# The opening of a fused attention and mixture kernel, with the order of each engine written out

## The chip, the cores and the metric

The kernel runs on one core of a Trainium2 chip. The metric is the device time of one execution in microseconds, lower is better. The time before the change is 762.0 us, the median of three runs (761.38 to 763.36). A core has TensorE (PE, matrix products and transposes), VectorE (DVE), ScalarE (ACT), GpSimd (POOL) and a sync engine (SP) that issues the DMAs. Each works through its own list in order and waits on semaphores where an input comes from another.

## The reference

Three layers in a row, all in fp32. Attention with keys and values pooled over 8 positions (8 batches, 8 heads, 576 positions, 64 wide), then a layer with squared relu, then a soft mixture of 8 experts:

```
k_p = k.reshape(B, H, Sp, 8, D).mean(axis=3)       # v_p likewise, Sp = 72
scores = scale * q @ k_p.T                          # per batch and head
attn = softmax(scores)
x = (attn @ v_p) as [4608 tokens, 512]
h = x @ w_in                                        # 512 x 2048, stored as 64-bit floats
x = relu(h)**2 @ w_out                              # 2048 x 512, 64-bit floats too
logits = x @ phi                                    # 512 x 32 slots
d = softmax(logits over tokens); slot_input = d.T @ x
slot_out[e] = relu(slot_input[e] @ w1[e]) @ w2[e]
out = softmax(logits over slots) @ slot_out
```

## The kernel before

Tokens are worked in 36 tiles of 128. Tile t goes through attention in steps: `att_qT` (four PE transposes of q, L218, copied by ACT, L222, into the one buffer `acc`), `att_sc` (scores on PE, L234; maxima on DVE, L241; eight exponentials with sums on ACT, L245; for tiles 2, 14 and a few others DVE subtracts, L250, and `att_exp` does one exponential, L259), `att_norm` (DVE, L264 to L268), `att_aT` (PE transposes, L299, two ACT copies, L300), and `att_av` (values on PE, L311; ACT copies the result as a rounded part `xh`, L318; DVE takes the rest as `xl`, L319).

The first layer is worked in units (t, j): tile t by quarter j of w_in (512 columns). A unit is 12 matmuls (L452) in two halves of six: per 128 rows kk of the quarter, high times high, high times low, and low times high, so kk 0 and 1 are the first half, 2 and 3 the second. After it come relu (L465) and square (L474) on ACT, or the square on DVE, and a store of g to DRAM.

w_in arrives as 64-bit floats. Each chunk (j, kk), 128 x 512, is converted by `conv_steps` in four steps: ACT L342; DVE L344, L347, L351; DVE L355, L356; ACT L394 (the rounded part) and POOL L395 (the rest). The buffer `tmp` has eight slots, so L342 of a chunk waits for L395 of the third chunk before it. The loads of a quarter go into one of two staging tiles (quarter 2 into that of 0, quarter 3 into that of 1), freed by L351.

A planner of the framework orders each engine's instructions by their place in the program and a timeline that it simulates; `early` raises a call's priority, `behind`, `pinned` and `paced` put a call's instructions behind a marked instruction on that instruction's engine. Such an edge is an order in a list and no wait on the chip. In `opening()`, before, tile 0's steps are early, conversions of quarters 0 and 1 are cut into steps and put behind marks, and tiles 1 to 3 follow with the planner's order. Units start with (0, 0), and 2u and 2u + 1 are the slots of unit u; `at(slot, ...)` hangs a call on a slot. From slot 2 on hang the conversions of quarter 2 (`CS`, each behind the latest relu on ACT), then those of quarter 3, at slots 12 to 18 the k poolings of batch 1 (`pool_k`, 32 PE matmuls each, L164), at 20 to 26 its V poolings on DVE, at 24 tile 4's attention. The V of batch 0 is pooled chunk by chunk: two of the four on PE (`pool_v`, L182) and two on DVE (`pool_v_dve`, L189).

SP's list at the start is k of batch 0 (four loads), q of tile 0, two chunks of w_in, v (four), two chunks of w_in, q of tile 1, four chunks of quarter 1, q of tiles 2 and 3.

## Time and profile before

| | us |
|---|---|
| median of three runs | 762.0 |
| the profiled execution | 760.21 |
| its span, from first to last instruction | 758.4 |
| PE busy in it | 718.1 (95%) |
| DVE busy | 532.6 (70%) |
| ACT busy | 391.0 (52%) |
| POOL busy | 131.3 (17%) |
| mean granted clock of PE | 0.985 |

The busy share of each engine over the whole span says which one is the bound on average. PE's 95% leaves some 40 us; 13 of them lie in the first 60 us and 14 in the last 58. What a change in one stage is worth is read in that stage, from the busy time in a window, the timeline there, and what an instruction waited for before it began (in square brackets: the idle time of its engine and what ended it). Busy times count an instruction from start to end; instructions of one engine overlap by some 0.1 us in a dense list.

### The profile page before, as it was taken

The page shows a single profiled execution, that of the slowest core. Times are in us where ns is not written, and L with a number is a line of the kernel's source. Part 1 is how long each engine was busy: PE and PEld are TensorE (multiplying, and loading weights), DVE is VectorE, ACT ScalarE, POOL GpSimd, SP SyncE. Part 2 cuts the span into 40 slices and gives each one's busy share as a digit, 9 for nine tenths or more (in the row PEclk, how much of TensorE's full clock was granted, in tenths as well). Part 3 has the DMA queues.
Part 4 walks back from the last instruction along what each step waited for, and adds up shares of the span by engine and source line. Part 5 has one row for each costly group of instructions (what it writes and reads, how often), then busy time and mean ns, then how long its engine had stood idle before and what let it go on. Part 6 is the DMA issues. An engine that isn't in the chain of part 4 may idle for free.

```text
span 758.4 us, 14481 instructions
## 1 busy us (share of the span) xinstructions
PE 718.1 (95%) x5260; PEld 508.1 (67%) x5260; DVE 532.6 (70%) x1065; ACT 391.0 (52%) x1135; POOL 131.3 (17%) x151
## 2 busy tenths in 40 slices
PE   7589999999999999999999999999999999998993
PEld 7467788787776767676667666666666676663462
DVE  4996865397796788888888887788788746324153
ACT  2675577464756446346646552636674454341142
POOL 2232300004872400050351311220000000000000
PEclk9799999999999999999999999999999999999996
DMA  8965764658876987695998788788586436979988
GB/s 252 277 225 175 229 178 133 208 155 247 223 217 168 260 252 196 205 281 148 253 267 232 206 232 242 205 244 233 163 277 197 122 101 235 417 248 367 370 298 297
DMA packets 224135, 175.10 MB, mean 231 GB/s; under 512 B 75072, under 2 KB 186688, under 8 KB 224064
## 3 DMA queue, kind: packets, MB, share of 16 engines
q1 hardware_dynamic: 224064, 174.17, 76.1%
q8 instruction: 42, 0.69, 0.4%
q14 instruction: 29, 0.24, 0.1%
HBM read 126.94 MB, written 47.19 MB: 230 GB/s over the span
## 4 chain that ended last, share of the span: by engine, by line
PE 64%; DVE 16%; DMA 9%; ACT 5%; issue 2%; SPq 2%; POOL 1%; DVEq 0%; ACTq 0%; POOLq 0%
PE l L452 40%; PE misc L632 3%; PE pl L540 3%; PE misc L1100 2%; ACT es L245 2%; PE gT L311 2%; PE l L1068 2%; PE att L311 2%; DMA kv<-in_k_dram 2%; DMA st<-in_moe_w_in_dram 2%; PE gT L234 2%; DVE aT L286 2%; PE att L540 1%; DMA out_dram<-o 1%; PE att L164 1%
## 5 line engine op out<-in xcount | busy, mean ns | idle before, releaser
L452 PE MATMUL l<-w,xh 128*128 128x512 f32 x1152 | 380.4, 410 | 7.0 <-ACT xh L318 2.9
L452 PEld LDWEIGHTS l<-w,xh 128*128 128x128 f32 x1152 | 208.8, 189 | 72.9 <-issue 16.3
L452 PE MATMUL l<-w,xl 128*128 128x512 f32 x576 | 230.7, 401 | 0.7 <-DVE xl L319 0.7
L465 ACT ACTIVATE r<-l 128x512 f32<-128x512 f32 x144 | 86.3, 603 | 162.7 <-PE l L452 154.7
L452 PEld LDWEIGHTS l<-w,xl 128*128 128x128 f32 x576 | 108.8, 189 | 28.7 <-issue 3.4
L157 POOL TENSOR_TENSOR kv<-kv 72x512 f32<-72x512 f32 x40 | 54.1, 1357 | 224.7 <-DMA kv<-in_v_dram 115.9
L284 ACT COPY aT<-turned 32x256 f32<-32x256 f32 (+1 forms) x168 | 67.8, 404 | 21.1 <-DVE turned L293 19.1
L472 DVE TENSOR_TENSOR g<-l,r 128x512 f32<-128x512 f32 x57 | 38.8, 680 | 23.3 <-ACT r L465 15.1
L515 DVE STREAM_TRANSPOSE turned<-turned 128x1024 f32<-128x1024 f32 x39 | 47.5, 1229 | 3.8 <-DMA turned<-g_dram 3.8
L245 ACT ACTIVATE es<-att,mx 128x72 f32<-128x72 f32 x120 | 36.7, 331 | 21.7 <-DVE mx L241 21.4
L286 DVE COPY aT<-turned 32x256 f32<-32x256 f32 (+1 forms) x120 | 42.8, 356 | 1.7
L245 ACT ACTIVATE es<-gT,mx 128x72 f32<-128x72 f32 x120 | 36.8, 331 | 10.9 <-DVE mx L241 10.9
L474 ACT ACTIVATE g<-r 128x512 f32<-128x512 f32 x54 | 34.5, 640 | 0.8
L395 POOL TENSOR_TENSOR w<-tmp,w 128x512 fp32r<-128x512 f32 x16 | 22.8, 1426 | 67.4 <-ACT w L394 61.4
L472 DVE TENSOR_TENSOR tmp<-l,r 128x512 f32<-128x512 f32 x33 | 22.5, 682 | 16.3 <-ACT r L465 14.1
L515 DVE STREAM_TRANSPOSE tmp<-tmp 128x1024 f32<-128x1024 f32 x25 | 30.2, 1221 | 4.7 <-DMA tmp<-g_dram 4.7
L158 POOL TENSOR_TENSOR kv<-kv 72x256 f32<-72x256 f32 x40 | 32.7, 824 | 0.9
L344 DVE TENSOR_SCALAR tmp<-tmp 128x512 uint32<-128x512 uint32 x32 | 16.6, 517 | 21.5 <-ACT tmp L342 21.3
L342 ACT ACTIVATE tmp<-st 128x512 f32<-128x512 f32 x32 | 21.5, 676 | 17.6 <-DMA st<-in_moe_w_in_dram 13.3
L268 DVE TENSOR_TENSOR es<-es,rs 128x576 f32<-128x576 f32 x36 | 29.6, 824 | 0.8
L245 ACT ACTIVATION_READ_ACCUMULATOR es<-gT,mx 128x1 f32 x120 | 26.1, 217 | 0.0
L245 ACT ACTIVATION_READ_ACCUMULATOR es<-att,mx 128x1 f32 x120 | 26.0, 217 | 0.0
(203 smaller groups left out, 1058.8 us busy)
## 6 DMA issues: line engine op xcount, KB each, us to landing
g_dram<-g SPq DMA_DIRECT2D x95, 256.0 KB
turned<-g_dram SPq DMA_DIRECT2D x39, 512.0 KB
w<-in_moe_w_dram SPq DMA_DIRECT2D x32, 512.0 KB
tmp<-g_dram SPq DMA_DIRECT2D x25, 512.0 KB
w<-in_moe_w_dram SPq DMA_DIRECT2D x6, 2048.0 KB
g_back<-g_dram SPq DMA_DIRECT2D x40, 256.0 KB
kv<-in_k_dram SPq DMA_DIRECT2D x32, 288.0 KB
kv<-in_v_dram SPq DMA_DIRECT2D x32, 288.0 KB
```

Source lines behind the costliest of these rows:

```text
L157: eng.tensor_tensor(out=x[:, :, 0:4], in0=x[:, :, 0:4], in1=x[:, :, 4:8], op=ALU.add)
L158: eng.tensor_tensor(out=x[:, :, 0:2], in0=x[:, :, 0:2], in1=x[:, :, 2:4], op=ALU.add)
L245: mark["es", t] = nc.scalar.activation(out=es[:, e], in_=sv[:, h], func=AF.Exp, bias=mx[:, e:e + 1], accum_out=rsum[:, t % 8, e, 0:1],)
L284: nc.scalar.copy(out=dst, in_=src)
L286: eng[e].tensor_copy(dst, src)
L311: nc.tensor.matmul(px[e * D:(e + 1) * D, i * P + off:i * P + off + n], vp_t[b][:, 2 * i + e], aT[:, 2 * i + e, off:off + n],)
L452: mm = mark["l1", t, j] = nc.tensor.matmul(hp_t[t, j], steps[i][0], steps[i][1], start=(i == 0), stop=(i == 2 * n - 1))
L465: nc.scalar.activation(out=r, in_=hp, func=AF.Relu, scale=1.0 / (R * R if sq == "V" else R))
L472: mark["sq"] = nc.vector.tensor_tensor(out=dst, in0=pre, in1=src, op=ALU.mult)
L474: nc.scalar.activation(out=dst, in_=src, func=AF.Square)
L515: nc.vector.transpose(out=gc.rearrange("p (n i) -> p n i", i=32), in_=gc.rearrange("p (n f) -> p n f", f=32))
L540: mark["logits"] = nc.tensor.matmul(pl[32 * c:32 * c + 32], a_sb[:, c, 32 * j:32 * j + 32], gT[:, c], start=(alone or j == 0), stop=(alone ...
```

## The change

`opening()` is written anew. A helper `do` runs a call and puts every instruction of it behind the last instruction that the call before left on the same engine, so each engine's list in the opening is the order of the text. In this text k is pooled before q of tile 0 is transposed; each chunk of quarters 0 and 1 is converted in steps between the attention steps of tiles 0 to 3; three V chunks are pooled on PE and one on DVE; the six warm-up matmuls behind the transposes of tile 0 go. The units (0, 0), (1, 0), (2, 0), (3, 0) are inside the opening, the slots 0 to 7 run after it, and the other units follow behind its last PE instruction, quarter by quarter up to (3, 2). The conversions of quarter 2 hang on slots 7, 8, 9 and 11 in place of 2, 5, 7 and 9. Of the loads, q of tile 1 goes ahead of the second two chunks of quarter 0, q of tile 2 ahead of quarter 1, q of tile 3 into its middle.

```diff
--- before.py
+++ after.py
@@ -56,7 +56,7 @@
     GO, LO = 3, 5
     PEP = (0, 1, 2)
     AE = "V" * 16
-    CS = ((2, 5, 7, 9), (13, 14, 15, 17))
+    CS = ((7, 8, 9, 11), (13, 14, 15, 17))
 
     const = ctx.enter_context(tc.tile_pool(name="const", bufs=1))
     wp = ctx.enter_context(tc.tile_pool(name="wp", bufs=4))
@@ -834,8 +834,8 @@
     a_at.update(zip(range(NT - 4, NT), (234, 236, 248, 253)))
 
     units = [
-        (0, 0), (0, 1), (1, 0), (3, 1), (3, 0), (1, 1), (2, 0), (0, 2),
-        (2, 1), (2, 2), (1, 2), (3, 2), (0, 3), (2, 3), (3, 3), (1, 3),
+        (0, 0), (1, 0), (2, 0), (3, 0), (0, 1), (1, 1), (2, 1), (3, 1),
+        (0, 2), (1, 2), (2, 2), (3, 2), (0, 3), (2, 3), (3, 3), (1, 3),
     ]
     units += [(t + u, j) for t in range(NI, NT, 2) for j in range(NQ) for u in range(2)]
 
@@ -906,10 +906,6 @@
         if b not in PEP:
             at(s0 - 4, make_kb, b)
 
-    def attention_now(t):
-        for fn in (att_qT, att_sc, att_exp, att_norm, att_aT, att_av):
-            fn(t)
-
     def make_constants():
         nc.vector.tensor_tensor(out=s4, in0=ident[:, 0:32], in1=ident[:, 32:64], op=ALU.add)
         nc.vector.tensor_tensor(out=s4, in0=s4, in1=ident[:, 64:96], op=ALU.add)
@@ -937,79 +933,113 @@
     load_w("in", 0, 0, 2)
     for i in range(NPAIR):
         load_kv(v, raw_v, 0, i)
+    load_q(1)
     load_w("in", 0, 2, 4)
-    load_q(1)
-    load_w("in", 1)
-
-    pk0 = ps("att")
-    for i in range(NPAIR):
-        pool_k_pe(pk0[:, i * SP:(i + 1) * SP], raw_k.pop((0, i)))
     load_q(2)
+    load_w("in", 1, 0, 2)
     load_q(3)
+    load_w("in", 1, 2, 4)
 
     def opening():
         conv = {(j, kk): conv_steps(j, kk) for j in range(PC) for kk in range(KD)}
-
-        def go(j, kk, n=4):
+        last = {}
+
+        def do(fn, *a):
+            traced = nc.cur_bb.bb.instructions
+            n = len(traced)
+            with ExitStack() as es:
+                for ins in last.values():
+                    es.enter_context(tc.issue_after(ins))
+                res = fn(*a)
+            for ins in traced[n:]:
+                last[ins.engine] = ins
+            return res
+
+        def go(j, kk, n=1):
             for _ in range(n):
-                next(conv[j, kk])
+                do(next, conv[j, kk])
 
         warm = ps1.tile([P, P], F32, tag="pl", name="warm")
         for _ in range(11):
-            nc.tensor.matmul(warm, ident, ident)
-        early(kb_from, 0, pk0)
+            do(nc.tensor.matmul, warm, ident, ident)
+        pk0 = ps("att")
+        for i in range(NPAIR):
+            do(pool_k_pe, pk0[:, i * SP:(i + 1) * SP], raw_k.pop((0, i)))
+        go(0, 0)
+        do(kb_from, 0, pk0)
+        do(att_qT, 0)
+        go(0, 0)
+        go(0, 1)
+        do(att_sc, 0)
         go(0, 0, 2)
-        early(att_qT, 0)
-        warm = ps1.tile([P, P], F32, tag="pl", name="warm")
-        for _ in range(6):
-            behind(["q0"], nc.tensor.matmul, warm, ident, ident)
-        go(0, 0, 1)
-        behind([("qT", 0), "kbA"], go, 0, 0, 1)
-        early(att_sc, 0)
-        go(0, 1, 1)
-        behind(["kbV"], go, 0, 1, 2)
-        behind([("es", 0)], go, 0, 1, 1)
-        early(att_norm, 0)
-        for i in range(0, NPAIR, 2):
-            behind([("sc", 0), ("es", 0)], pool_v, 0, i, kvp)
-            behind([("mx", 0) if i == 0 else ("norm", 0)], pool_v_dve, 0, i + 1, kvp)
-        go(0, 2, 1)
-        behind([("mx", 0)], go, 0, 2, 2)
-        behind([("es", 0)], go, 0, 2, 1)
-        early(att_aT, 0)
-        early(att_av, 0)
-        go(0, 3, 3)
-        behind([("aT", 0)], go, 0, 3, 1)
-        for half in range(2):
-            l1_half(0, 0, half)
-        behind(["pv"], att_qT, 1)
-        behind([("aT", 0)], att_sc, 1)
-        att_norm(1)
-        behind([("l1", 0, 0)], att_aT, 1)
-        att_av(1)
-        for t in (2, 3):
-            att_qT(t)
-            for kk in range(2):
-                if t == 3:
-                    go(1, kk)
-            att_sc(t)
-            att_exp(t)
-            att_norm(t)
-            att_aT(t)
-            for kk in range(2, 4):
-                if t == 3:
-                    go(1, kk)
-            att_av(t)
-
-    opening()
+        do(pool_v, 0, 0, kvp)
+        do(pool_v, 0, 1, kvp)
+        go(0, 1)
+        do(att_norm, 0)
+        go(0, 1)
+        do(pool_v_dve, 0, 3, kvp)
+        do(att_aT, 0)
+        go(0, 1)
+        do(att_qT, 1)
+        do(pool_v, 0, 2, kvp)
+        go(0, 2, 2)
+        do(att_av, 0)
+        go(0, 3)
+        do(att_sc, 1)
+        go(0, 2, 2)
+        do(l1_half, 0, 0, 0)
+        go(0, 3)
+        do(att_norm, 1)
+        go(0, 3)
+        do(att_qT, 2)
+        do(att_aT, 1)
+        go(0, 3)
+        go(1, 0)
+        do(att_sc, 2)
+        go(1, 0)
+        do(att_av, 1)
+        do(l1_half, 0, 0, 1)
+        do(att_exp, 2)
+        do(att_norm, 2)
+        go(1, 0, 2)
+        go(1, 1)
+        do(l1_half, 1, 0, 0)
+        do(att_qT, 3)
+        do(att_aT, 2)
+        go(1, 1)
+        do(l1_half, 1, 0, 1)
+        do(att_sc, 3)
+        do(att_av, 2)
+        go(1, 1, 2)
+        go(1, 2, 2)
+        do(l1_half, 2, 0, 0)
+        do(att_norm, 3)
+        do(l1_half, 2, 0, 1)
+        do(att_aT, 3)
+        go(1, 2, 2)
+        go(1, 3, 2)
+        do(att_av, 3)
+        do(l1_half, 3, 0, 0)
+        do(l1_half, 3, 0, 1)
+        go(1, 3, 2)
+        return last[mark["l1", 3, 0].ins.engine]
+
+    opened = opening()
     nc.sync.dma_start(out=phi_sb, in_=phi.rearrange("(k p) s -> p k s", p=P))
     at(5, load_q, 4)
     at(17, load_q, 5)
+    for u in range(NI):
+        for half in range(2):
+            run_slot(2 * u + half)
     for u, (t, j) in enumerate(units):
         for half in range(2):
-            if u:
+            if u == NI:
+                with tc.issue_after(opened):
+                    l1_half(t, j, half)
+            elif u > NI:
                 l1_half(t, j, half)
-            run_slot(2 * u + half)
+            if u >= NI:
+                run_slot(2 * u + half)
         if j == NQ - 1:
             x_t.pop(t)
     for s in sorted(ev):
```

## Rows read from the trace of the kernel before

**Rows 1.** Windows: stretch, then busy us of PE, PEld, DVE, ACT, POOL, clock, DMA, GB/s

```profile
11.10:60.30 49.20, 37.71 (x325) 29.65 (x321) 45.96 (x81) 31.46 (x94) 13.95 (x10) 0.90 0.82 245
60.30:91.80 31.50, 31.50 (x215) 23.86 (x216) 24.73 (x46) 16.77 (x32) 7.56 (x5) 1.00 0.64 196
...
20.00:30.00 10.00, 5.29 (x26) 4.15 (x28) 8.58 (x15) 7.33 (x27) 2.81 (x2) 0.66 0.92 297
```

**Rows 2.** Windows of line L452 alone, same columns

```profile
0.00:60.20 60.20, 12.28 (x36) 7.13 (x36) 0.91 0.81 243
60.20:95.00 34.80, 29.49 (x116) 21.31 (x117) 1.00 0.68 212
```

**Rows 3.** Chain that ended last, one piece: start, us, what

```profile
60.27 5.80 PE l L452 x24
```

**Rows 4.** Timeline of the first 23 us: start, us, engine, line, [idle before, releaser]

```profile
6.08 0.96 PE L164 MATMUL att<-ident,kv 72*64 72x72 f32 x22
8.96 0.66 PE L218 MATMUL gT<-ident,qt 128*128 128x128 f32 x4 [1.92 <-DMA qt<-in_q_dram]
9.55 3.59 PE L164 MATMUL att<-ident,kv 72*64 72x72 f32 x106
10.40 0.69 ACT L342 ACTIVATE tmp<-st 128x512 f32<-128x512 f32 x1 [8.17 <-DMA st<-in_moe_w_in_dram]
13.98 0.44 DVE L195 TENSOR_SCALAR kb<-att 64x288 f32<-64x288 f32 x1
20.01 0.66 ACT L342 ACTIVATE tmp<-st 128x512 f32<-128x512 f32 x1 [4.44 <-DMA st<-in_moe_w_in_dram]
22.05 1.11 PE L218 MATMUL att<-ident,qt 128*128 128x128 f32 x4 [2.33 <-DMA qt<-in_q_dram]
```

**Rows 5.** Timeline: normalisation of tiles 0, 2; exponentials and xl of tile 3

```profile
27.10 0.74 DVE L268 TENSOR_TENSOR es<-es,rs 128x576 f32<-128x576 f32 x1
...
49.44 0.32 ACT L245 ACTIVATE es<-att,mx 128x72 f32<-128x72 f32 x1
...
51.55 0.75 DVE L268 TENSOR_TENSOR es<-es,rs 128x576 f32<-128x576 f32 x1
51.73 0.24 ACT L245 ACTIVATION_READ_ACCUMULATOR es<-att,mx 128x1 f32 x1
...
59.59 0.69 DVE L319 TENSOR_TENSOR xl<-att,xh 128x512 fp32r<-128x512 f32 x1 [1.18 <-ACT xh L318]
```

**Rows 6.** Timeline: the last chunk of quarter 3

```profile
91.06 0.68 DVE L356 SCALAR_TENSOR_TENSOR tmp<-tmp 128x512 uint32<-128x512 uint32 x1
92.47 1.28 POOL L395 TENSOR_TENSOR w<-tmp,w 128x512 fp32r<-128x512 f32 x1 [2.82 <-ACT w L394]
```

**Rows 7.** Timeline: pieces of a conversion, a held L344, V pooled on PE and DVE

```profile
11.12 0.43 DVE L344 TENSOR_SCALAR tmp<-tmp 128x512 uint32<-128x512 uint32 x1 [8.01 <-ACT tmp L342]
...
13.37 0.69 DVE L356 SCALAR_TENSOR_TENSOR tmp<-tmp 128x512 uint32<-128x512 uint32 x1
...
16.06 3.66 PE L182 MATMUL l<-kv,ident 72*72 72x128 f32 x32
17.78 1.90 DVE L189 TENSOR_REDUCE vp<-kv 72x128 f32<-72x1024 f32 x1
...
40.18 0.62 ACT L394 CAST w<-tmp 128x512 fp32r<-128x512 f32 x1 [0.53 <-DVE tmp L356]
40.88 1.39 POOL L395 TENSOR_TENSOR w<-tmp,w 128x512 fp32r<-128x512 f32 x1 [1.95 <-ACT w L394]
41.40 1.15 DVE L344 TENSOR_SCALAR tmp<-tmp 128x512 uint32<-128x512 uint32 x1
```

**Rows 8.** Timeline of PE before 60.2 us

```profile
56.41 0.66 PE L218 MATMUL gT<-ident,qt 128*128 128x128 f32 x4
...
58.62 1.17 PE L164 MATMUL att<-ident,kv 72*64 72x72 f32 x32
59.62 0.66 PE L234 MATMUL gT<-kb,acc 128*64 128x144 f32 x4
```

## The prediction, made before the changed kernel was run

> **What bounds the kernel now.** I read the stretches first: engine busy time by window. From 60.3 us PE is busy in all of 31.50 us, and it stays nearly so; before, from 11.1 to 60.3 us, it is busy in 37.71 of 49.20 us, while DVE is busy in 45.96 [rows 1]. So the opening is set by DVE, with ACT and POOL in its chains, and after it the kernel is a PE stream in which a microsecond won early is worth a microsecond at the end. The change touches the opening and the first 13 units only, so the question is when PE has done a given amount of work. I take the end of the thirteenth unit, (0,3) in both orders: 36 layer-one matmuls lie before 60.2 us and 116 between 60.2 and 95.0 us [rows 2]; with a few records missing that is 13 x 12 = 156 at about 95 us. At full rate 24 in a row take 5.80 us [rows 3], so a unit of 12 takes 2.8 us and its tail.
>
> Then the timeline of the opening. ACT takes its second-half chunk of w_in at 20.01 us after 4.44 us idle, and the exponentials of tile 0 stand behind it; the transposes of tile 1 wait until 22.05 us for q [rows 4]. The normalisation of tile 0 starts at 27.10 us, that of tile 2 at 51.55 [rows 5]. But little DVE time is lost by it: its queue holds conversion and attention mixed finely, and it idles 49.20 - 45.96 = 3.2 us up to 60.3 and 31.50 - 24.73 = 6.8 us up to 91.8 us [rows 1], when the last chunk of w_in's last quarter (quarter 3) is converted: L356 at 91.06, POOL's subtraction done at 92.47 + 1.28 = 93.75 us [rows 6]. Unit (0,3) uses that chunk in its last three matmuls, at about 94.3. So DVE's ledger up to 91.7 us, not PE's, is close behind the time of unit (0,3).
>
> **The change, part by part.** (1) All k pooling stands before q's transposes. Now PE waits 1.92 us for q at 8.96 and then pools the last 106 matmuls in 3.59 us, so kb is at 13.98 [rows 4]. At 34 ns each, 128 matmuls from 6.08 us, where they begin now, end at 10.5 us: kb 3.3 us earlier, at the time at which the first chunk arrives (10.40) [rows 4].
>
> (2) q of tile 1 is loaded ahead of the second half of w_in quarter 0. Tile 1's transposes no longer wait to 22.05; the chunk that landed at 20.01 [rows 4] lands 1 to 1.5 us later (an estimate: 256 KB at the 245 GB/s of the opening [rows 1] are 1.1 us). ACT comes to it at 21.9 in the written order, so this costs nothing there; with 1.5 us more it would cost 0.6. q of tiles 2 and 3 lies between chunks of quarter 1, which ACT wants only after 32 us: covered.
>
> (3) The exponentials of tile 0 no longer stand behind that chunk. Walking the written lists of PE, ACT, DVE and POOL one by one with the durations of [rows 3 to 7] and their like, each instruction starting when its engine's previous one and its inputs are done, I get the normalisations of tiles 0 and 2 done at 18.4 and 38.6 us, against 27.84 and 52.30 now [rows 5]. The same walk over the order of before gives tile 3's xl at 59.45 us; the trace has 59.59 [rows 5]. In the walk tile 0's scores follow kb and q's copy at 12.1, its maxima end at 13.8; four DVE steps and the norm, held by POOL, give 18.4. PE then does its transposes, those of q 1 and a V chunk to 21.6; V's copy, L342 (22.6), three steps, xl of tile 0, two maxima, two steps, three steps (28.2), and tile 1's norm, held again: 30.2. Transposes and copies, L394 and L395 of the last chunk of quarter 0 (33.8), three matmuls, relu, square and tile 2's exponential (36.6), sum and norm of tile 2: 38.6. So far a gain of 9 to 14 us.
>
> (4) From there the written order gives it back. Each conversion is ACT L342, three DVE steps, two DVE steps, ACT L394, POOL L395. The order puts L342 of the next chunk behind L394 of the last one, and L394 waits for DVE's last step. So DVE stands from the end of L356 through L394 (0.62) and L342 (0.69): 1.35 us, three times [rows 4, 7]. Its next step L344 then falls into POOL's subtraction of the chunk before, which the trace shows to hold it: 1.15 us instead of 0.41, ending 0.28 us after POOL's [rows 7]; some 0.6 us, three times. And tile 3's scores stand before tile 2's values: xh of tile 2 queues on ACT behind eight exponentials (49.44 to 51.97 us for tile 3 now, 2.5 us [rows 5]), with xl behind it on DVE: 2.9 us of DVE idle. The chain, from tile 2 normalised at 38.6: two DVE steps 1.4, L394+L342 1.3, three stalled DVE steps 2.1, first maximum 0.4 (43.7); exponentials and xh 3.1, xl 0.7, two steps 1.4 (48.8); L394+L342 1.3, three steps 2.1, norm of tile 3 1.1 (53.3); transposes and two copies 1.6, L394+L342 1.2, three steps 2.1, xl of tile 3 0.7 (58.8); ten matmuls 2.4: unit (3,0), the last of the opening, ends at 61.2 us. Sum of the DVE gaps over 0.15 us in the walk: 10.0 us, against 3.2 now.
>
> What is that worth? At 60.2 us PE has now done three units, one batch-1 k pooling (32 matmuls, 1.1), and tile 4's transposes and half its scores (1.0, of 1.3 with their tails) [rows 8]. One unit more and without those 2.1 it would stand at 60.2 + 2.8 - 2.1 = 60.9. So the opening itself comes out even: 61.2 against 60.9.
>
> (5) One V reduction goes from DVE (1.90 us) to PE, 16 matmuls of the 32 that take 3.66 us, 1.8 us [rows 7]: DVE gains 1.9, and PE's 1.8 lie in its waits. The warm-up matmuls that go lie in a wait too. If PE's waits were gone, they would cost and give those times.
>
> (6) Conversion of quarter 2 is moved: now two of its chunks are done in the opening (ten L395 lie before 60.3, eight of them of quarters 0 and 1 [rows 1]); in the change ACT may take the first only behind the relu of unit (3,0), at about 62.5 us, and DVE has nothing written from 60.0 to 63.2. So DVE owes two chunks, 2 x (2.94 + 0.5) = 6.9 us [rows 7], in a stretch that has 6.8 us idle now. The ledger of DVE up to the last chunk of quarter 3: 80.6 us now, of which 10.0 idle. In the change: 70.6 - 1.9 work, 10.0 idle in the opening, 3.2 before quarter 2, and 0 to 3 of the 6.8 after that, since the pace by relus stays. That is 81.9 to 84.9, so 1.3 to 4.3 us later than now, of which unit (0,3) has some 0.6 in hand: 0.7 to 3.7 us later.
>
> Who waits: unit (0,1) also waits some 1.2 us for the last chunk of quarter 1, whose L394 is written behind relu and square of unit (3,0); this lies inside the same delay. SP: the loads of quarter 3 need the staging tile that quarter 1 frees at 58 us in the walk; they queue in front of batch-1 v loads, but its first use is after 70 us. No cost, unless v is held, then DVE pooling moves later and the upper end holds.
>
> PE's clock: now it is at 0.66 of full rate in 20 to 30 us [rows 1], around waits such as the 2.33 us before 22.05 [rows 4]. In the walk PE waits 3.6, 3.8, 3.0 and 3.3 us (before tile 1's transposes, unit (2,0), tile 3's transposes, unit (3,0)), so half rate (1.2 of 2.4 GHz) is likely in some of it. Bounds: 0, if it falls only beside waits, to 3.3 us (two matmul groups in the chain of tile 2, two transposes, half of unit (3,0)). I take 0.5. The Trainium skill (TensorE: Matmul & The Clock Gate, section HAM oscillation) says that waits between short bursts of matmuls put the array back to half rate again and again; it speaks against this order, and by it the upper end would stand: rival (c).
>
> Whether L268 is held by POOL as L344 is, no row of the opening shows, as none starts inside an L395; in the walk those of tiles 0 and 1 do. Bounds 0 and 0.74 each, the latter by L344's row [rows 7], which is the nearest and which I take; without it unit (3,0) ends 1.6 us earlier, at 59.6. The Trainium skill (SBUF — State Buffer, section Who interferes with whom) says that a DVE instruction with two inputs in SBUF waits for the whole of a GpSimd instruction that reads SBUF; by it 61.2 stands, without it 59.6.
>
> Middle of 0.7 to 3.7, with 0.5 for the clock: 2.7 us later at unit (0,3). After it PE is the bound, so it is kept. Against the profiled execution, 758.4 us span in 760.2 us, this is 762.9; the median of the runs, 762.0, lies 1.8 above that execution, so I forecast 762.0 + 2.7 = 764.7 us.
>
> **Rivals.** (a) About the same. Work of batch 1 that the written order doesn't pin (four k poolings of 1.1 us on PE, its V pooling on DVE) slips into the gaps of the opening. Then DVE's 10.0 idle shrinks by up to 5, and PE has three poolings less to do after unit (3,0). For it: the gaps are wider than such a piece. Against: the V loads need a buffer that the k poolings free. -2 to +1.5 us: 760 to 763.5, at 762.
>
> (b) Faster. The head start of 9 to 14 us survives, since the stalls of (4) are smaller than walked, or DVE's order is not as written: DVE idles no more than now in the opening, 3.2. Then the ledger is 1.9 less work and 6.8 less idle than in (6): 4 to 7 us earlier; the PE side allows it (unit (3,0) at 54). 755 to 758.5, at 757. For it: tile 2 is 14 us ahead at 38 us. Against: the walk reproduces the present order to 0.14 us.
>
> (c) Slower by more. The clock's upper end and the late relu add: 2.7 + 2.8, and tile 4's V pooling late: 767 to 770. It decides if PE is at half rate when unit (3,0) starts.
>
> (d) The order isn't followed, so nothing changes beside the units' order: 762 within 1.
>
> **How the numbers follow.** Forecast 764.7 (762.7 to 766.7) 0.38, (a) 0.24, (b) 0.22, (c) 0.10, (d) 0.06. The range of 757 to 768.5 leaves out the lower half of (b) and some of (c), under 0.2. About 0.3% (2.3 us) is what a measurement of this kernel can tell from no change. Above 764.3 lie 0.24 of the forecast's share and (c): slower 0.34. Below 759.7 lie nearly all of (b) and a little of (a): faster 0.23. The rest, 0.43, is within.
>
> **What would show it.** Right: tile 2 normalised near 38 to 40 us, xl of tile 2 only near 47, unit (3,0) from about 59 us; DVE idle some 10 us between 11 and 60; last L395 of w_in after 95 us. Wrong: unit (3,0) done before 57 us, or batch-1 pooling between 38 and 58 us. If the last L395 comes late and the span doesn't grow, the ledger wasn't the bound.

## The result, and the profile after

| | before | after |
|---|---|---|
| median of the runs | 762.2 us | 771.2 us (770.1 to 771.6) |
| ratio, 95% interval | 1 | 1.0112, 1.0083 to 1.0141 |
| span of the profiled execution | 758.4 us | 769.9 us |
| last L395 of w_in done, in it | 93.75 us | 107.0 us |

The change costs 9 us; the forecast was +2.7 and its range ended at 768.5. The windows of after come first, in the columns of [rows 1]; the last three stretches are added.

```profile
11.10:60.30 49.20, 36.11 (x264) 29.66 (x265) 34.94 (x63) 29.52 (x90) 8.67 (x7) 0.90 0.68 200
60.30:91.80 31.50, 28.82 (x196) 20.60 (x192) 24.12 (x51) 13.99 (x33) 8.40 (x6) 0.95 0.66 208
60.00:70.00 10.00, 8.50 (x53) 6.35 (x50) 5.30 (x11) 3.20 (x7) 1.00 (x2) 0.83 0.68 239
90.00:100.00 10.00, 7.69 (x29) 5.64 (x30) 8.52 (x18) 6.90 (x26) 4.50 (x2) 0.83 0.90 244
91.80:110.00 18.20, 16.64 (x80) 12.93 (x80) 12.54 (x22) 12.62 (x41) 7.11 (x5) 0.91 0.92 276
```

The last of these stretches in the kernel before:

```profile
91.80:110.00 18.20, 18.11 (x125) 14.37 (x125) 11.51 (x25) 15.25 (x52) 1.28 (x1) 1.00 0.79 241
```

The opening lost little: PE is busy in 36.11 of 49.20 us where it was in 37.71, at the same clock of 0.90, and the 1.92 us wait ahead of 11.1 us [rows 4] is gone. The loss lies behind it. From 60.3 to 91.8 us PE was busy all the time at full rate; now it lacks 2.68 us and runs at 0.95, and to 110 us another 1.56 us at 0.91. That is 4.2 us idle and at most 0.05 x 31.5 + 0.09 x 18.2 = 3.2 us of half rate: 7.4 of the 11.5 us between the two spans. The V pooling that is now PE's is not among them, since all of it lies ahead of 60.2 us. Behind 110 us PE is idle for 27.7 us where it was for 24.8; the last 1.2 us are not assigned. The windows of L452 alone say when, beside [rows 2]:

```profile
0.00:60.20 60.20, 11.35 (x36) 7.05 (x36) 0.91 0.70 209
60.20:95.00 34.80, 24.77 (x84) 16.24 (x84) 0.93 0.69 217
95.00:106.00 11.00, 8.42 (x35) 6.60 (x36) 0.90 0.88 253
```

Both kernels have issued 36 matmuls by 60.2 us. Before had 152 by 95 us, after has 120, and 155 only by 106: unit (0,3) is some 11 us later. About 2 us of these are scores and transposes of the attention (L234 x8 and L299 x8) that PE now does ahead of 106 us and did behind 95 us before.

DVE's timeline of the opening (start, us, engine, line, idle before and what ended it), beside [rows 5] and the held L344 of [rows 7]:

```profile
16.79 1.47 DVE L268 TENSOR_TENSOR es<-es,rs 128x576 f32<-128x576 f32 x1
...
30.10 1.59 DVE L268 TENSOR_TENSOR es<-es,rs 128x576 f32<-128x576 f32 x1
...
41.23 0.76 DVE L268 TENSOR_TENSOR es<-es,rs 128x576 f32<-128x576 f32 x1
...
44.58 1.04 DVE L344 TENSOR_SCALAR tmp<-tmp 128x512 uint32<-128x512 uint32 x1 [1.26 <-ACT tmp L342]
...
50.39 0.69 DVE L319 TENSOR_TENSOR xl<-gT,xh 128x512 fp32r<-128x512 f32 x1 [2.75 <-ACT xh L318]
...
61.79 0.68 DVE L319 TENSOR_TENSOR xl<-att,xh 128x512 fp32r<-128x512 f32 x1
...
67.89 0.43 DVE L344 TENSOR_SCALAR tmp<-tmp 128x512 uint32<-128x512 uint32 x1 [3.95 <-ACT tmp L342]
...
70.90 0.69 DVE L157 TENSOR_TENSOR kv<-kv 72x512 f32<-72x512 f32 x1 [1.57 <-DMA kv<-in_v_dram]
```

The stalls are those that were walked: L344 behind L342 (1.26 us idle, then 1.04 instead of 0.41), xl of tile 2 behind xh (2.75). The row at 67.89 was in the ledger of (6): quarter 2 starts only behind the relu of unit (3,0), 3.95 us idle where 3.2 were taken. The last row was not: DVE's queue then stands at L157, the pooling of batch 1's V, whose data is not there. SP's queue says why:

```profile
61.94 1.77 SPq L372 DMA_DIRECT2D st<-in_moe_w_in_dram  x4
63.81 0.55 SPq L150 DMA_DIRECT2D kv<-in_v_dram  x1
```

The four loads of quarter 3 wait for the staging tile, which quarter 1's last L351 frees at 61.9 us; the V load behind them would have found its buffer free at 60.4, when the k pooling at 59.20 ended. DVE's windows up to the last L356 of quarter 3, before and then after in its three parts (columns: busy, count, clock, DMA, GB/s):

```profile
11.10:91.74 80.64, 70.63 (x126) 0.94 0.75 226
```

```profile
11.10:60.30 49.20, 34.94 (x63) 0.90 0.68 200
60.30:67.89 7.59, 3.57 (x7) 0.78 0.65 219
67.89:104.94 37.05, 32.22 (x64) 0.95 0.75 223
```

So DVE is idle for 14.3 us in the opening, 4.0 up to the start of quarter 2 and 4.8 behind it, 23.1 in all where before had 10.0; its work is 70.7 us in both. Of the 4.8 us, 3.1 are waits of L157 for V (1.57, 0.78 and 0.72). Before waited for V too, 2.83 and 0.83 us.

POOL and PE show where the late conversions arrive, the last chunk of quarter 1, of quarter 2 and of quarter 3:

```profile
69.52 1.29 POOL L395 TENSOR_TENSOR w<-tmp,w 128x512 fp32r<-128x512 f32 x1 [9.00 <-ACT w L394]
...
89.95 3.21 POOL L395 TENSOR_TENSOR w<-tmp,w 128x512 fp32r<-128x512 f32 x1 [3.42 <-ACT w L394]
...
105.68 1.33 POOL L395 TENSOR_TENSOR w<-tmp,w 128x512 fp32r<-128x512 f32 x1 [1.29 <-ACT w L394]
```

```profile
59.20 1.17 PE L164 MATMUL att<-ident,kv 72*64 72x72 f32 x32
...
62.53 0.50 PE L452 MATMUL l<-w,xl 128*128 128x512 f32 x1 [1.50 <-DVE xl L319]
...
93.22 0.50 PE L452 MATMUL l<-w,xh 128*128 128x512 f32 x1 [2.17 <-POOL w L395]
```

### The profile page after: what moved, and what is told of

Its sections match the earlier page's. It is cut to its first block, busy times and chain, and to the rows that moved or that the text cites. A ratio compares the mean times of both kernels' runs of the same rounds, so it can differ in the third digit from the quotient of the medians.

```text
span 769.9 us, 14492 instructions
## 1 busy us (share of the span) xinstructions
PE 722.7 (94%) x5264; PEld 510.8 (66%) x5264; DVE 527.5 (69%) x1064; ACT 391.3 (51%) x1136; POOL 132.1 (17%) x151
## 4 chain that ended last, share of the span: by engine, by line
PE 65%; DVE 14%; DMA 9%; ACT 6%; issue 3%; POOL 1%; SPq 1%; ACTq 0%; DVEq 0%; POOLq 0%
PE l L452 39%; PE misc L632 3%; PE pl L540 2%; DMA turned<-g_dram 2%; PE misc L1130 2%; DMA g_dram<-tmp 2%; PE gT L234 2%; PE att L311 2%; PE l L1098 2%; PE att L234 2%; ACT aT L284 2%; PE gT L311 2%; DVE es L268 2%; ACT es L245 1%; DMA out_dram<-o 1%
## 5 line engine op out<-in xcount | busy, mean ns | idle before, releaser
L452 PE MATMUL l<-w,xh 128*128 128x512 f32 x1152 | 381.6, 411 | 8.4 <-DVE tmp L472 3.3
L452 PEld LDWEIGHTS l<-w,xh 128*128 128x128 f32 x1152 | 208.5, 189 | 74.9 <-issue 16.0
L452 PE MATMUL l<-w,xl 128*128 128x512 f32 x576 | 231.4, 402 | 1.9 <-DVE xl L319 1.9
L452 PEld LDWEIGHTS l<-w,xl 128*128 128x128 f32 x576 | 109.1, 189 | 31.6 <-issue 3.6
L157 POOL TENSOR_TENSOR kv<-kv 72x512 f32<-72x512 f32 x40 | 53.1, 1332 | 228.4 <-DMA kv<-in_v_dram 120.3
L286 DVE COPY aT<-turned 32x256 f32<-32x256 f32 (+1 forms) x120 | 38.1, 318 | 1.6
L395 POOL TENSOR_TENSOR w<-tmp,w 128x512 fp32r<-128x512 f32 x16 | 24.2, 1511 | 79.3 <-ACT w L394 78.0
L344 DVE TENSOR_SCALAR tmp<-tmp 128x512 uint32<-128x512 uint32 x32 | 16.4, 512 | 30.1 <-ACT tmp L342 30.1
L268 DVE TENSOR_TENSOR es<-es,rs 128x576 f32<-128x576 f32 x36 | 35.0, 973 | 0.9
L342 ACT ACTIVATE tmp<-st 128x512 f32<-128x512 f32 x32 | 21.6, 677 | 11.8 <-DMA st<-in_moe_w_in_dram 7.9
L632 PE MATMUL misc<-g,d 128*32 128x512 f32 x134 | 24.2, 597 | 2.8 <-DVE d L619 2.3
```

The costliest lines, as they stand in the source:

```text
L157: eng.tensor_tensor(out=x[:, :, 0:4], in0=x[:, :, 0:4], in1=x[:, :, 4:8], op=ALU.add)
L268: mark["norm", t] = nc.vector.tensor_tensor(out=es, in0=es, in1=rs.unsqueeze(2).to_broadcast([P, H, SP]), op=ALU.mult)
L286: eng[e].tensor_copy(dst, src)
L452: mm = mark["l1", t, j] = nc.tensor.matmul(hp_t[t, j], steps[i][0], steps[i][1], start=(i == 0), stop=(i == 2 * n - 1))
L632: mark["dg"] = nc.tensor.matmul(dp[32 * j:32 * j + 32], d[:, u], g if t < NT - 4 else natural(g), start=(u == 0), stop=(u == width(t) - 1),)
```

## The experiments

The theories: ORDER (the stalls of the written order), CLOCK (PE at half rate behind its waits), LATE V (SP's queue), LATE CONVERSION (quarter 2 begins too late), and the parts of the change each by itself. "After" and "before" below are the two kernels; each ratio is against before on the same chip, where its executions lay between 757 and 770 us.

**V first.** After, with one load moved:

```
-    at(3, load_w, "in", 3)
...
-            at(s0 - 10 + 2 * i, load_kv, v, raw_v, b, i)
+            if (b, i) != (1, 0):
+                at(s0 - 10 + 2 * i, load_kv, v, raw_v, b, i)
...
+    def v_then_w():
+        load_kv(v, raw_v, 1, 0)
+        pinned("kv", load_w, "in", 3)
+
+    at(12, v_then_w)
```

> The changed kernel with SP's order alone altered after the opening: the first V load of batch 1 stands ahead of the four loads of quarter 3, which wait for the staging tile; in the changed kernel it stood behind them and landed at 70.9 us. Its place in DVE's queue (ahead of quarter 2's conversions, behind the opening) stays. Theory LATE V: L157 starts at 62 to 65 us instead of 70.9, the chunks of quarter 2 leave POOL 2 to 3 us earlier, and the kernel takes 767 to 769 us (ratio 1.006 to 1.009). Theory LATE CONVERSION (the relu of unit (3,0) at 67 us and what follows it set the pace, V is beside the path): L157 starts earlier and the time stays within 1 us of 771 (1.011). Theory CLOCK: no change of the time beyond what other half-rate stretches give.

Measured 767.2 us, 1.0059 (1.0036 to 1.0083). SP's queue, then PE's windows (columns: busy, count, clock, DMA, GB/s):

```profile
62.23 0.33 SPq L150 DMA_DIRECT2D kv<-in_v_dram  x1
62.66 1.77 SPq L372 DMA_DIRECT2D st<-in_moe_w_in_dram  x4
```

```profile
60.30:91.80 31.50, 31.50 (x233) 0.91 0.74 232
91.80:110.00 18.20, 17.08 (x110) 1.00 0.72 216
```

The V load is issued 1.6 us earlier, ahead of 2 MB, and its pooling starts 5 us earlier, while DVE waits for the relu of unit (3,0) in any case:

```profile
65.90 0.69 DVE L157 TENSOR_TENSOR kv<-kv 72x512 f32<-72x512 f32 x1 [1.65 <-DMA kv<-in_v_dram]
```

The second chunk of quarter 2 leaves POOL at 77.0 us instead of 80.0, and PE has no idle time from 60.3 to 91.8 us. LATE V stands: about half of the loss. An earlier form of this edit, which let V be loaded at 24 us into a third buffer, shows the danger:

```
-            at(s0 - 10 + 2 * i, load_kv, v, raw_v, b, i)
+            at(11 if (b, i) == (1, 0) else s0 - 10 + 2 * i, load_kv, v, raw_v, b, i)
```

> The changed kernel with one load moved: the first V load of batch 1 is issued three slots earlier, ahead of quarter 3's loads on SP's queue, so that it no longer waits for the staging tile of quarter 1. Theory LATE V: DVE's V pooling of batch 1 no longer waits for data at 70.9 us (1.57 us, and 0.78 and 0.72 after it), the conversions of quarter 2 behind it on DVE's queue come 2 to 3 us earlier, and the kernel takes 768 to 769 us instead of 771. Theories CLOCK, ORDER and LATE CONVERSION (the conversions are late for the relu, not for V): DVE's wait moves elsewhere, 770.5 to 771.5.

Measured 780.6 us, 1.0229. The expectation missed that the pooling moves up with its load, into the middle of the opening, where DVE waits for it:

```profile
33.50 0.69 DVE L157 TENSOR_TENSOR kv<-kv 72x512 f32<-72x512 f32 x1 [11.41 <-DMA kv<-in_v_dram]
```

**The order.** After, with the first edit at three places and the second at one:

```
-        go(1, 0, 2)
-        go(1, 1)
+        go(1, 0)
+        go(1, 1)
+        go(1, 0)
...
-        do(att_sc, 3)
         do(att_av, 2)
+        do(att_sc, 3)
```

> The changed kernel with two of its written steps in another order: the first ACT step (L342) of the next chunk of quarter 1 ahead of the last ACT step (L394) of the chunk before, three times, and the values of tile 2 ahead of the scores of tile 3. Theory ORDER (the stalls of DVE that the written order makes, 1.35 us three times and 2.75 us, are what was lost): unit (3,0) ends 2 us earlier with the clock as it is, up to 4 if a half-rate stretch goes with a wait; 767 to 769 us. Theory CLOCK: the DVE gaps shrink, but PE still waits as long before its bursts, half-rate stretches remain as many, unit (3,0) within 1 us of 65.5: 770 to 772. Theory LATE V: DVE still stands until the V of batch 1 is loaded; quarter 3's loads follow the last L351 of quarter 1, some 1 to 2 us earlier: 769.5 to 770.5.

Measured 770.2 us, 1.0083 (1.0050 to 1.0116). The opening is 2.4 us shorter, and DVE then waits for V until it is nearly as late as in after (70.90):

```profile
59.40 0.68 DVE L319 TENSOR_TENSOR xl<-att,xh 128x512 fp32r<-128x512 f32 x1
70.25 0.69 DVE L157 TENSOR_TENSOR kv<-kv 72x512 f32<-72x512 f32 x1 [8.71 <-DMA kv<-in_v_dram]
```

Both together:

> Both alterations together: the next chunk's L342 ahead of the last chunk's L394 and the values of tile 2 ahead of the scores of tile 3 (alone: unit (3,0) ended 3 us earlier, and all of it was lost again by 96 layer-one matmuls, behind V at 70.5 us; 1.008), and the first V load of batch 1 ahead of quarter 3's loads. Theory TWO COVERS (opening's stalls and late V each hide the other): the opening's 3 us now reach the end, last subtraction of quarter 3 at 101 to 103 us instead of 107, 764 to 766 us (1.002 to 1.005). Theory LATE CONVERSION alone: the paced conversions follow the relu, which is 3 us earlier, 767 (1.006 to 1.008). If neither: as with the order alone, 1.008.

Measured 767.7 us, 1.0054 (1.0023 to 1.0085). No better than V alone: ORDER was worth nothing that these runs can tell, with V late or early, since the intervals overlap in both pairs.

**Quarter 2 set free.** After, with the wait for a relu taken from the conversions of its first two chunks:

```
-            at(CS[j - 2][kk], paced, conv_in, j, kk)
+            if (j, kk) in ((2, 0), (2, 1)):
+                at(7, conv_in, j, kk)
+            else:
+                at(CS[j - 2][kk], paced, conv_in, j, kk)
```

> The changed kernel with the conversions of the first two chunks of quarter 2 free of their wait for the last relu, so that they may run in the opening's gaps, as two of them do in the kernel before. Theory LATE CONVERSION: two chunks of about 3.4 us of DVE work lie in gaps of the opening, the last subtraction of quarter 3 ends at 100 to 102 us instead of 107.0, and the kernel takes 764 to 767 us. Theory CLOCK: the steps fall between those of tiles 2 and 3 and lengthen the opening by as much as they bring, waits before unit (3,0) are longer: 770 to 773. Theory LATE V: the conversions are ahead of the V pooling, so its wait no longer holds them: 766 to 768, with the V pooling itself still at about 70 us.

Measured 776.6 us, 1.0158 (1.0100 to 1.0215): no gain, with DVE 5.01 us at L157. The same edit with V first, and with V first and the order:

> The changed kernel with the V load ahead of quarter 3's loads (alone: 1.0059) and the first two chunks of quarter 2 without their wait for a relu; the written order is the change's. Theory LATE CONVERSION: the chunks fill the gaps that the written order leaves on DVE (14 us idle from 11 to 60 us), 0.998 to 1.003. Theory ORDER: their steps stand in front of tile 3's, unit (3,0) is later by as much as they take, 1.005 to 1.010.

> The changed kernel with all three alterations: L342 ahead of L394 and the values of tile 2 ahead of the scores of tile 3; the first V load of batch 1 ahead of quarter 3's loads; the first two chunks of quarter 2 without their wait for a relu, so that they may fill DVE's gaps in the opening. The first two gave 1.0054 together, the third alone 1.0158 with V still late. Theory LATE CONVERSION: with V out of the way the two chunks (some 7 us of DVE) come forward, the last subtraction of quarter 3 ends at 96 to 100 us, and the kernel is at 0.997 to 1.001. Theory ORDER (DVE's list in the opening is what matters, and more in it only delays tiles 2 and 3): 1.006 to 1.012.

Measured 771.6 us, 1.0134 (1.0103 to 1.0164), and 769.6, 1.0105 (1.0075 to 1.0136). The first is slower than V first alone (1.0036 to 1.0083). The second one's DVE, behind the two chunks:

```profile
77.46 0.23 DVE L171 TENSOR_SCALAR kb<-att 64x72 f32<-64x72 f32 x1 [5.92 <-PE att L164]
```

The idle time only moved: DVE's queue now stands at the copy of batch 1's kb, which PE pools behind its units. All four chunks free (`if j == 2:` in the edit), with V first and the order:

> The changed kernel with the two alterations of the order, the first V load of batch 1 ahead of quarter 3's loads (these alone 1.0054), and now all four chunks of quarter 2 without their wait for a relu. With two of them free (1.0105) those two came 3 to 4 us earlier, and then DVE stood 5 to 9 us until the third, whose L342 waits for the relu of unit (0,1) at 75 us: the third left POOL at 86 us in both. Theory PACE (the third and fourth chunk wait for relus of units which themselves wait for the last chunk of quarter 1): the third leaves POOL before 80 us, the last of quarter 3 at 95 to 100 us, 0.998 to 1.004. Theory ORDER (each early conversion step on DVE and ACT stands before a step of tile 3 or of the last chunk of quarter 1): unit (3,0) and (0,1) later still, 1.008 to 1.014. Theory CLOCK: the time goes with the half-rate stretches of the execution, whatever the conversions do: PE's idle time falls, the half-rate loss stays at 7 to 8 us, 1.005 to 1.010.

Measured 769.8 us, 1.0073 (1.0044 to 1.0103). The third chunk did leave POOL at 74.1 us, but the last of quarter 3 only at 103.1. As the cause of what is left in this change LATE CONVERSION is not borne out: no form of the edit gained. But each form also puts its steps into DVE's list ahead of others, so the theory isn't excluded.

**The end of quarter 1.** After with this edit; then with V first; then with the order too:

```
+        go(1, 3, 2)
         do(l1_half, 3, 0, 0)
         do(l1_half, 3, 0, 1)
-        go(1, 3, 2)
```

> The changed kernel with one written step moved: the end of the last chunk of quarter 1 (its L394 on ACT and L395 on POOL) ahead of unit (3,0) instead of behind its relu and square. In the changed kernel this chunk left POOL at 71.1 us, though DVE had its last input at 62.2, unit (0,1) had its relu at 75.2, and the third chunk of quarter 2 is paced by that relu. Theory PACE: the chunk leaves POOL at 64 to 66 us, the relu of unit (0,1) comes 2 to 5 us earlier, V still late: 1.006 to 1.010. Theory V: nothing moves while V holds DVE at 70 us, 1.010 to 1.012.

> The step moved and the V load first, the rest of the order as in the change (V first alone: 1.0059, last chunk of quarter 1 at 71.4 us). Theory PACE: 1.001 to 1.004. Theory OPENING: 1.004 to 1.007.

> The same step moved, together with L342 ahead of L394, the values of tile 2 ahead of the scores of tile 3, and the first V load of batch 1 ahead of quarter 3's loads (these without the step: 1.0054, last chunk of quarter 1 at 68.2 us, relu of unit (0,1) at 72.1). Theory PACE: chunk at 62 to 64 us, relu of unit (0,1) at 68 to 69, each later conversion 2 to 4 us earlier, 1.000 to 1.003. Theory OPENING (the waits of PE in the opening and the half rate behind them are what is left): 1.004 to 1.006 as without it.

Measured 1.0145 (1.0101 to 1.0189), 1.0085 (1.0055 to 1.0115) and 1.0056 (1.0032 to 1.0081). The chunk left POOL at 65 to 67 us and the relu of unit (0,1) came 2.6 to 5.7 us earlier than without the edit, much as expected, and there was no gain. The theory PACE fell.

**The clock.** After, with 39 matmuls on the identity in PE's waits, at six places like this:

```
+        for _ in range(9):
+            do(nc.tensor.matmul, warm, ident, ident)
         do(att_aT, 1)
```

> The changed kernel with 39 small matmuls on the identity (no result uses them) put into PE's waits of the opening: 4 before the transposes of tile 0, 9 before those of tile 1, 2 before those of tile 2, 9 before unit (2,0), 7 before those of tile 3, 8 before unit (3,0). The changed kernel's trace shows four stretches of 3.4 us at half rate in the opening (18.9, 32.5, 42.8, 63.2 us), each behind such a wait. Theory CLOCK (the time lost in the opening beyond the forecast is PE at half rate): granted clock 1.0 from 20 to 66 us, unit (3,0) ends at 61 to 62 us instead of 65.5, and the kernel takes 767 to 768 us instead of 771. Theory LATE CONVERSION (what sets the end is quarter 2, begun behind the relu of unit (3,0), and the DVE ledger): unit (3,0) also ends earlier, and since the conversions are paced by that relu the whole gain is passed on, 767.5. Theory LATE V (the loads of batch 1's V behind those of quarter 3 hold DVE to 70.9 us): unit (3,0) earlier, but quarter 3's loads wait for the last L351 of quarter 1 at 61.2 us, which the clock moves by 2 us at most: 769 to 771.

Measured 773.2 us, 1.0143 (1.0090 to 1.0196). The windows of the profiled execution, which took 778.65 us:

```profile
11.10:60.30 49.20, 40.89 (x275) 0.90 0.71 200
60.30:91.80 31.50, 29.67 (x251) 1.00 0.59 180
91.80:110.00 18.20, 15.84 (x74) 1.00 0.94 292
```

From 60 us on the clock stays full, and PE is idle there for 1.83 + 2.36 us, as in after (2.68 + 1.56): those waits are not the clock's. What a full clock saves can't be read from this run, since the 39 cost 10.7 us of PE in it, and the relu of unit (3,0) came at 68.8 us instead of 66.7. (Unit (3,0) of after ended at 66.7 us, not at the 65.5 that the expectations name.)

**Parts of the change in before.** The loads of q in their new places (as the change's diff has them); the same with all k pooling ahead of q's transposes; that pooling alone; and one more reduction of V on PE, alone:

```
-        early(att_qT, 0)
+        early(behind, ["pk"], att_qT, 0)
...
-            behind([("mx", 0) if i == 0 else ("norm", 0)], pool_v_dve, 0, i + 1, kvp)
+            behind([("mx", 0) if i == 0 else ("norm", 0)], pool_v if i == 0 else pool_v_dve, 0, i + 1, kvp)
```

> The kernel before with one part of the change alone: the loads of q of tiles 1 to 3 in their new places among the chunks of w_in; opening, units and conversions as before. Theory ORDER, CLOCK, LATE V and LATE CONVERSION alike put no cost on the loads: within 0.3% of the kernel before (0.997 to 1.003), or a gain of 1 to 3 us if the 2.33 us wait of PE for q of tile 1 was on the path. Theory LOADS (the chunks that come later for q cost the DVE ledger): 1.002 to 1.005.

> The kernel before with two parts of the change: the pooling of k before q's transposes, and the loads of q of tiles 1 to 3 in their new places (alone: 1.0037, with PE at half rate from 10.1 to 20.4 us in the profile). Theory CLOCK: the cost of the loads was that half-rate stretch, which started behind the wait for q of tile 0 before any moved load was issued; without the wait 0.995 to 1.000. Theory LOADS (the later chunks of w_in cost DVE's ledger): 1.002 to 1.005 as alone.

> The kernel before with the change's first part alone: all pooling of k stands before q's transposes on PE, so that PE no longer waits 1.92 us for q in the middle of it. Executions of the kernel before differ (758 to 767 us on this chip) and two kernels built on it showed PE at half rate from 9 or 10 us for 10 us, behind that wait, with kb at 17.5 us instead of 14.7. Theory CLOCK: without the wait the half-rate stretch at 9 us goes, kb is at 11 to 12 us in each execution, and the median falls by 1 to 4 us: 0.995 to 0.999. Theory LEDGER (DVE's queue sets the opening's end, kb 3 us earlier only makes tile 0's steps stand earlier in it): 0.998 to 1.001. Rival on the other side: q's transposes, now behind k, come later, and the planner's list shifts: 1.002 to 1.005.

> The kernel before with one part of the change alone: one of the two V reductions of batch 0 goes from DVE (1.9 us) to PE and ACT. Prediction's term (5): DVE has 1.9 us less in a stretch in which it idles 3.2 of 49 us, so up to 1.9 us earlier at unit (0,3): 0.9975 to 1.000. Rival: the sixteen matmuls and the copy lie ahead of tile 0's values on PE and ACT, and the gain goes: 0.999 to 1.002.

Measured 1.0037 (1.0008 to 1.0066), 1.0031 (0.9995 to 1.0066), 1.0016 (0.9991 to 1.0040) and 1.0075 (1.0049 to 1.0102). The k pooling is near nothing. The loads alone have an interval just above 1; a cost of theirs is neither shown nor excluded, as their execution went to half rate early, too (see the last section). The last edit surprises; its windows, and its k pooling beside [rows 4]:

```profile
11.10:60.30 49.20, 42.78 (x338) 0.81 0.81 243
60.30:91.80 31.50, 31.50 (x227) 0.89 0.52 162
91.80:110.00 18.20, 18.20 (x95) 1.00 0.90 271
```

```profile
10.14 6.74 PE L164 MATMUL att<-ident,kv 72*64 72x72 f32 x106
```

PE is busier in the opening than before (42.78 against 37.71 us) and gets no further, 36 matmuls of L452 by 60.2 us, at a clock of 0.81 instead of 0.90. The k pooling takes 6.74 instead of 3.59 us, and nothing of the edit lies ahead of it. So in this execution part of the loss goes with the clock and not with the edit; that all four executions (766.9 to 768.2 us) lie above the longest of the 13 of before on that chip (766.5) speaks against its being all. How much is the edit's own stays open.

**The units.** Before, with the change's `units`, and with or without its slots of quarter 2's conversions:

```
-    CS = ((2, 5, 7, 9), (13, 14, 15, 17))
+    CS = ((7, 8, 9, 11), (13, 14, 15, 17))
```

> The kernel before with another part of the change alone: the order of the first units quarter by quarter (all four tiles' first quarter in the opening), with the slots of the conversions of quarter 2 that go with it; opening not written out, loads as before. Theory LATE CONVERSION and LATE V (which come from the units' order and not from the written order): most of the loss is here, 1.006 to 1.012, with quarter 3's loads and V behind the last chunk of quarter 1, as in the changed kernel. Theory ORDER and CLOCK (the stalls of the written order): 0.997 to 1.003.

> The kernel before with the new order of units alone, and the conversions of quarter 2 in the slots of before (2, 5, 7, 9) instead of the changed kernel's (7, 8, 9, 11). With the new slots the units alone gave 1.0119: the opening ended as early as before, the last chunk of quarter 1 left POOL at 49 us, and DVE stood until the relu of unit (3,0) at 65.7 us before it began quarter 2 (first L351 at 67.5 us, before 54). Theory LATE CONVERSION (the later slots of quarter 2 are the loss, and the units only call for them): first L351 of quarter 2 before 60 us, 1.002 to 1.006. Theory UNITS (the units' order itself: quarter 1 and 2 follow at once for four tiles, so conversions are wanted earlier than DVE can give them): 1.009 to 1.012, PE waiting for POOL's subtractions at 75 to 105 us.

Measured 772.4 us, 1.0119 (1.0092 to 1.0146), and 764.8 us, 1.0038 (1.0011 to 1.0066). The windows of the first, then of the second:

```profile
60.30:91.80 31.50, 28.81 (x203) 1.00 0.62 187
91.80:110.00 18.20, 15.43 (x86) 0.81 0.68 211
```

```profile
60.30:91.80 31.50, 31.50 (x248) 1.00 0.61 192
91.80:110.00 18.20, 18.20 (x107) 1.00 0.78 241
```

The same text of the opening, the same units; with the new slots PE is idle for 2.69 + 2.77 us behind 60 us, and at 0.81 of the clock in the later stretch; with the old ones it has neither. The timeline of the first shows what DVE does instead:

```profile
58.93 0.69 DVE L319 TENSOR_TENSOR xl<-att,xh 128x512 fp32r<-128x512 f32 x1 [4.42 <-ACT xh L318]
...
66.78 0.43 DVE L344 TENSOR_SCALAR tmp<-tmp 128x512 uint32<-128x512 uint32 x1 [1.69 <-ACT tmp L342]
```

Quarter 1 was done at 49.1 us there, V came at 63.6, and quarter 2 still began at 66.8 us, behind the relu of unit (3,0). So this is a whole loss of the size of the change's, from the units with their slots, with neither the written order nor V behind quarter 3's loads (they are issued at 43.1 us there, V at 59.9). With the old slots one chunk of quarter 2 is converted in the opening and leaves POOL at 54.3 us; its tile 3 is 2.9 us later for it (xl at 61.79) and the kernel is the faster one. The written opening with the units of before was not run.

## Why the prediction was wrong, point by point

(1) was right: kb starts at 10.34 us (10.5). (2) holds in this trace: the moved chunk's L342 starts at 23.49 us, behind a copy of V that waited for PE, and not behind its load. What the loads cost by themselves is open (1.0037, 1.0008 to 1.0066).

(3) was right up to tile 1. The normalisations end at 18.3 and 31.7 us (18.4 and 30.2, the second 1.5 late); tile 2's at 42.0 against 38.6. L268 is held by POOL as taken: 1.47 and 1.59 us where an L395 runs, 0.76 where none does. The Trainium skill (SBUF — State Buffer, Who interferes with whom) was right here.

(4) was right in mechanism and in the size of the stalls: the gaps were walked at 1.35, three times, and 2.9 us, and are 1.26, 1.25, 1.60 and 2.75. The sum was too small: DVE's idle time in the opening was to be 10.0 us and is 14.3, xl of tile 3 was to start at 58.1 us (58.8 less its 0.7) and starts at 61.79, and unit (3,0) was to end at 61.2 us and its relu starts at 66.71. The walk is at full rate; in this execution PE's granted clock was 0.50 from 18.6 to 22.0, 32.3 to 35.7, 42.5 to 45.9 and 63.0 to 66.4 us, the lower of its two levels. A pair of L452, in unit (3,0) and behind it:

```profile
64.02 1.06 PE L452 MATMUL l<-w,xh 128*128 128x512 f32 x2
...
66.51 0.63 PE L452 MATMUL l<-w,xh 128*128 128x512 f32 x2
```

At half rate PE loses at most half of such a stretch, 1.7 us; the three ahead of xl could cost up to 5.1 us, and it is 3.7 late (an estimate from these rows). So the term of the clock was mis-sized: 0.5 us was taken, and its upper end, 3.3, was nearer. This is argued from the rows, not shown by a run. The Trainium skill (TensorE: Matmul & The Clock Gate, HAM oscillation) spoke for the upper end, and the trace agrees with it: each of the four stretches stands behind a wait of PE (1.61, 3.85, 1.98 and 1.50 us). Not each wait brought one: behind those of 1.66 and 2.48 us, before 50.41 and 56.93, the clock stayed at 1.00.

"The opening itself comes out even" was right up to 60.2 us: PE's idle time is the same, and 36 matmuls stand there in both. It was not right for the end of unit (3,0), 66.7 us, where before would stand at 60.2 + 2.8 = 63.0: xl made PE wait 1.50 us, and most of the unit ran at half rate.

(5) is open: 1.9 us less on DVE were to bring a gain of up to that much, and alone the edit cost 0.75%. How much of that is the clock of its executions isn't shown. That PE's 1.8 us lie in its waits agrees with after's opening.

(6) is the step that failed. Its ledger of DVE from 11.1 us to the last L356 of quarter 3 was 68.7 us of work, 10.0 idle in the opening, 3.2 before quarter 2 and 0 to 3 behind it: 81.9 to 84.9. Measured are 70.7, 14.3, 4.0 and 4.8, so 93.8 us; and unit (0,3), forecast 0.7 to 3.7 us later, was some 11 later. The largest miss, 4.3 us, is the opening's idle time of (4). The next is the idle time behind the start of quarter 2, 4.8 us, 3.1 of them waits for V. The sentence on SP named the hazard, loads of quarter 3 in front of batch 1's V, and priced it at no cost since V's first use is late. But V's pooling stands in DVE's queue ahead of quarter 2's steps: the user that counts is the conversion behind it. Taking V out of the way gained in each of four pairs: 1.0112 to 1.0059, 1.0083 to 1.0054, 1.0158 to 1.0134 and 1.0145 to 1.0085, so 0.2 to 0.6%; only the first pair's intervals don't overlap (they meet at 1.0083). In that pair it is some 4 of the 9 us.

Of the rivals (c), at a chance of 0.10, came nearest: V's pooling was late, and unit (3,0) ran at half rate from its fourth matmul on. Even its 770 us was short. (a) had one thing right: a k pooling of batch 1 lay in a gap, at 59.20 us; but so it did before, at 58.62 [rows 8]. (b)'s lead, still 10 us when tile 2 was normalised, was spent by 60 us, and (d) fell, since the order was followed.

What stays open is the other half. With V first and the order's stalls gone 0.5% remain, and the runs that freed quarter 2 or finished quarter 1 earlier didn't bring it back. PE's half rate behind 60 us is of this size in after; no run isolates it. The units with their slots alone lose as much as the whole change, in the other opening. No version beat before.

## What to carry to other kernels

When a load stands in a queue behind loads that wait for a buffer, look up what its consumer has queued behind itself on its own engine; that, and not the load's first use, prices the delay. Work that is paced by an event must be costed from where the event now lies: with one and the same order of units, in the opening of before, moving quarter 2's conversions from slots (2, 5, 7, 9) to (7, 8, 9, 11) cost 0.8%. And an order that shortens a chain is worth only what the next wait behind it lets through: of 2.4 us won in the opening 0.65 were left ten microseconds later.

## What the runs showed of the hardware that was not expected

The clock isn't set by the program alone. The kernel before first went to half rate at 22.1 us; with the same PE instructions up to the k pooling, the two with the loads and with V's reduction did so at 10.0 and 9.0 us, behind the same wait for q (1.82 and 1.74 us against 1.92), and stayed there for 10.2 us, so that kb began at 17.14 and 16.92 us instead of 13.98. The kernel before alone spread from 757 to 770 us over its later executions; only medians of several tell 0.3% apart. And an L395 on POOL took from 1.26 us to 3.21, the latter while six of DVE's steps ran beside it at their usual 0.28 to 0.68 us (89.95 us): in that row POOL, and not DVE, was the one that took longer.
